# Blocked causal attention and token/channel mixer: neighbouring weight rows in one partition, every fourth channel in a chunk, and down projections that wait for their own third

## The chip, the cores and the metric

The kernel runs on one core of one Trainium2 chip. The metric is the device time of one execution in microseconds (us); medians are over several executions. All executions told of here are in the undisturbed ("fast") state, at a granted TensorE clock of 0.995 to 1.000 over the whole span. Beside the device time there is the span, from the first to the last instruction in the trace.

Engines: PE is TensorE (PEld its weight loads), DVE is VectorE, ACT is ScalarE, POOL is GpSimd, SP is SyncE. In this kernel PE's matmuls write into PSUM banks, and a bank is given to the next ones when DVE or ACT has read it out ("evacuated" it); in the trace before PE waits 0.6 us at two places where L507 needs a bank that x_sb (DVE) still has to read out. "Packed" weights have their columns side by side; with a step of 4 every fourth column is taken. The prediction uses the line numbers of the kernel before.

## The reference

```python
# q, k, v: (8, 8, 576, 64) drawn with standard deviation 0.1
def _attn_ref(q, k, v):
    scores = np.matmul(q, k.transpose(0, 1, 3, 2)) / np.sqrt(D)
    mask = block_i >= block_j                    # blocks of 64 positions
    scores = np.where(mask, scores, -1e9)
    attn = softmax(scores)
    return np.matmul(attn, v)

def _moe_ref(x, w_tok1, w_tok2, w_ch1, w_ch2):   # x: (8, 576, 512)
    xt = x.transpose(0, 2, 1)
    h = np.maximum(xt @ w_tok1, 0.0) @ w_tok2    # 576 -> 256 -> 576
    u = x + h.transpose(0, 2, 1)
    h2 = np.maximum(u @ w_ch1, 0.0) @ w_ch2      # 512 -> 1536 -> 512
    return u + h2
```

The heads of the attention, side by side, are the rows of x. Inputs and output are float32; the kernel multiplies in bfloat16.

## The kernel before

The kernel does not fix the order of its instructions by hand. It describes some thousand pieces of work with an engine, an estimated cost, dependencies and a priority. A list schedule then deals them out: whenever an engine is free on paper, it takes the piece of best priority whose dependencies are done on paper. The instructions are emitted in that order. In the trace before each engine's instructions start in the emitted order (by their lines, all 3029 matmuls of PE, 372 instructions of DVE and 234 of ACT), and PE's listed waits, 4.9 us in all, are each for a tile that DVE or ACT had to write or read.

```python
# costs of the plan, in us
def act_cost(n):          return 0.08 + n * 0.000833
def dve_cost(n, speed=1): return 0.09 + n * 0.00104 / speed
...
rc = P.add("DVE", 0.12, emit_rc, ...)                                # reciprocal of the row sums
mu = P.add("DVE", dve_cost(320), emit_mu, [rc], ..., give=[bank])    # x_sb, frees a PSUM bank
...
op = P.add("DVE", 0.02 + 32 * (k1 - k0) * 0.00185, emit, ...)        # transposes of q and k
...
def channel_up(b, uT_done, wc1_ready, prio):       # twelve chunks of 128 channels
    for cc in range(NDC):
        def emit(o, cc=cc, bank=bank):
            for m in range(NDM):
                nc.tensor.matmul(out=bank_of(bank),
                    lhsT=wc1_sb[:, m, 128 * cc : 128 * (cc + 1)],
                    rhs=uT[b % 2][:, :, m, :], start=(m == 0), stop=(m == NDM - 1))
        ...
        done.append(P.add(EVAC, evac_cost(512), emit, [op], prio, give=[bank]))   # relu into gT, DVE or ACT
...
def channel_down(b, g_done, wc2_ready, u_done, prio, mixed=False):
    ...
                for part in range(3):              # four of the twelve chunks each
                    ...
                        for cc in range(4 * part, 4 * part + 4):
                            nc.tensor.matmul(out=ps, lhsT=gt[:, cc, c0 : c0 + 128],
                                rhs=wc2_sb[:, cc, cols], ...)
                    deps = [prev] + (g_done + wc2_ready + u_done if part == 0 else [])
```

For batch 0 the first part also adds u by four matmuls with the identity (L950). In the last line a down projection depends on all twelve evacuations before its first third may start.

The softmax here doesn't subtract the row's maximum and nothing guards it: scores larger than these inputs give would overflow.

## Time and profile before

| | us |
|---|---|
| three runs before the change | 310.43 median (310.27 to 311.03) |
| six runs, three of them beside the changed kernel | 311.01 median (310.27 to 311.34) |
| span of the profiled run | 309.2 |

First the weight loads of the up projection, from the page's costliest groups (line, engine, operation, shape, count, then total us and mean ns of one). All are packed, and one takes 98 ns:

```profile
L874 PEld LDWEIGHTS <-wc_sb 128*128 128x128 bf16 x384 | 36.0, 98 | 44.5 <-issue 3.6
```

Second, DVE's timeline after batch 1's token mixing (start, length, work). The four sums u, which free PSUM banks and release the transposes on PE, run back to back with the fifth (um). The transposes of k and q, 1.23 to 1.26 us each, come after:

```profile
60.67 2.48 DVE L803 TENSOR_TENSOR u_sb<-mm,x_sb 128x512 bf16<-128x512 f32 x4 [2.05 <-PE mm L782]
63.19 0.69 DVE L803 TENSOR_TENSOR um_sb<-mm,x_sb 64x512 bf16<-64x512 f32 x1
...
64.76 1.26 DVE L349 STREAM_TRANSPOSE kT<-kraw 128x576 int32<-128x576 int32 x1
65.86 1.23 DVE L349 STREAM_TRANSPOSE qT<-qraw 128x576 int32<-128x576 int32 x1
```

### The profile page before, as it was taken

Reading aid. Unit: us, or ns where it says so; the run is one execution under the profiler, and the core shown is the slowest. Engines: PE = TensorE matmul, PEld = TensorE weight load, DVE = VectorE, ACT = ScalarE, POOL = GpSimd, SP = SyncE. Lnnn points to the kernel's source line nnn. Section 1 sums busy time; section 2 is a strip of 40 time slices with the busy share of each in tenths; the row PEclk is TensorE's granted clock in tenths of the full one; section 3 lists DMA queues with packets and bytes.
Section 4 is the critical chain, followed back from the end, with each engine's and each line's share of the span. In section 5 each row is a group of like instructions: output and inputs, shape, how many; then the busy total and the mean of one; then the engine's idle time right before and its main releaser. Section 6 shows DMA issues by size and latency. Waiting matters only on the chain.

```text
span 309.2 us, 7176 instructions
## 1 busy us (share of the span) xinstructions
PE 300.4 (97%) x3029; PEld 155.4 (50%) x3029; DVE 157.6 (51%) x372; ACT 165.8 (54%) x235; POOL 63.1 (20%) x96
## 2 busy tenths in 40 slices
PE   7999989999999999999999999999999999999995
PEld 3575436463556554554544556544444644444643
DVE  6967648796786497496557634525015012011021
ACT  5886864767876745758555776214603602613600
POOL 7956345611612511500220000000000000000000
PEclk9999999999999999999999999999999999999999
DMA  8999999998796996941291005104221312103004
GB/s 241 193 194 206 220 211 183 225 161 169 61 138 125 120 182 146 159 29 23 49 163 70 2 0 70 70 0 122 46 89 68 68 69 72 32 10 126 2 16 156
DMA packets 57024, 33.13 MB, mean 107 GB/s; under 512 B 43872, under 2 KB 47584, under 8 KB 56992
## 3 DMA queue, kind: packets, MB, share of 16 engines
q0 software_dynamic: 36960, 18.52, 45.6%
q1 hardware_dynamic: 19744, 13.57, 17.3%
q8 instruction: 23, 0.38, 0.5%
q10 hardware_dynamic: 288, 0.59, 0.5%
q14 instruction: 9, 0.07, 0.1%
HBM read 35.85 MB, written 9.44 MB: 146 GB/s over the span
## 4 chain that ended last, share of the span: by engine, by line
PE 85%; DMA 5%; DVE 4%; POOL 3%; ACT 1%; issue 1%; POOLq 0%
PE mm L958 30%; PE mm L874 26%; PE sc L460 8%; PE mm L507 7%; PE mm L782 5%; PE mm L688 5%; PE mm L901 4%; DMA qraw<-in_q_dram 3%; DMA kraw<-in_k_dram 2%; DVE x_sb L535 1%; ACT e_sb L479 1%; POOL gT L378 1%; DVE qT L349 1%; DVE kT L349 1%; POOL wc_sb L416 1%
## 5 line engine op out<-in xcount | busy, mean ns | idle before, releaser
L479 ACT ACTIVATE e_sb<-sc 128x1024 bf16<-128x1024 f32 x95 | 92.4, 1024 | 35.5 <-PE sc L460 34.9
L958 PE MATMUL mm<-wc_sb,gT 128*128 128x512 bf16 (+1 forms) x396 | 89.6, 373 | 0.0
L874 PE MATMUL mm<-uT,wc_sb 128*128 128x512 bf16 x384 | 88.6, 380 | 0.0
L674 ACT ACTIVATE gT<-mm 128x512 bf16<-128x512 f32 x75 | 44.8, 597 | 66.8 <-PE mm L874 66.6
L981 DVE TENSOR_TENSOR o_sb<-mm,u_sb 128x512 f32<-128x512 f32 (+1 forms) x29 | 19.5, 672 | 85.8 <-PE mm L958 85.8
L874 PEld LDWEIGHTS <-wc_sb 128*128 128x128 bf16 x384 | 36.0, 98 | 44.5 <-issue 3.6
L958 PEld LDWEIGHTS <-gT 128*128 128x128 bf16 x396 | 36.7, 98 | 41.3 <-issue 3.6
L460 PE MATMUL sc<-qT,kT 32*128 32x320 bf16 (+4 forms) x744 | 35.8, 281 | 2.7 <-DVE qT L349 1.6
L507 PEld LDWEIGHTS <-e_sb 128*128 128x128 bf16 x896 | 30.8, 97 | 9.3 <-issue 4.5
L507 PE MATMUL mm<-v,e_sb 128*128 128x65 bf16 x896 | 32.8, 193 | 1.1 <-DVE x_sb L535 0.6
L378 POOL DMA_DIRECT2D v<-in_v_dram x30 | 25.5, 869 | 39.8 <-PE sc L460 22.8
L535 DVE TENSOR_TENSOR x_sb<-mm,rinv 128x320 bf16<-128x320 f32 x64 | 30.4, 488 | 1.4
L460 PEld LDWEIGHTS <-kT 32*128 32x128 bf16 x752 | 12.8, 93 | 22.2 <-issue 19.3
L676 DVE TENSOR_SCALAR gT<-mm 128x512 bf16<-128x512 f32 x21 | 14.5, 690 | 15.3 <-PE mm L874 15.3
L349 DVE STREAM_TRANSPOSE kT<-kraw 128x576 int32<-128x576 int32 (+1 forms) x20 | 20.0, 1031 | 4.1 <-PE sc L460 2.9
L803 DVE TENSOR_TENSOR u_sb<-mm,x_sb 128x512 bf16<-128x512 f32 x28 | 17.4, 683 | 6.7 <-PE mm L782 6.7
L349 DVE STREAM_TRANSPOSE qT<-qraw 128x576 int32<-128x576 int32 (+1 forms) x20 | 20.0, 1025 | 0.7 <-DMA qraw<-in_q_dram 0.5
L688 PE MATMUL mm<-x_sb,w_sb 128*128 128x512 bf16 (+1 forms) x102 | 17.9, 316 | 0.3 <-DVE x_sb L535 0.3
L485 DVE MEMSET e_sb<- 64x128 uint32 (+1 forms) x72 | 10.6, 153 | 15.0 <-ACT e_sb L479 11.6
L782 PE MATMUL mm<-aT,w_sb 128*128 128x512 bf16 x72 | 17.0, 380 | 0.0
L329 POOL DMA_DIRECT2D kraw<-in_k_dram x15 | 8.4, 557 | 38.0 <-DVE kT L349 31.1
L529 DVE RECIPROCAL rinv<-mm 128x5 f32<-128x5 f32 x64 | 10.6, 180 | 9.2 <-PE mm L507 9.0
(68 smaller groups left out, 186.0 us busy)
## 6 DMA issues: line engine op xcount, KB each, us to landing
out_dram<-o_sb SPq DMA_DIRECT2D x15, 512.0 KB, 2.8
kraw<-in_k_dram POOLq DMA_DIRECT2D x15, 288.0 KB, 6.3
qraw<-in_q_dram POOLq DMA_DIRECT2D x15, 288.0 KB, 7.1
v<-in_v_dram POOLq DMA_DIRECT2D x24, 128.0 KB, 5.1
wc_sb<-in_moe_w_ch_dram POOLq DMA_DIRECT2D x8, 192.0 KB, 7.7
wc_sb<-in_moe_w_ch_dram POOLq DMA_DIRECT2D x3, 512.0 KB, 10.2
out_dram<-o_sb SPq DMA_DIRECT2D x10, 128.0 KB, 2.4
gT<-in_v_dram POOLq DMA_DIRECT2D x9, 128.0 KB, 6.1
```

What stands on the lines that cost most here:

```text
L349: nc.vector.transpose(dst[:, 0:S, :] .rearrange("p s e -> p (s e)") .bitcast(I32) .rearrange("p (a k) -> p k a", k=NB)[:, k0:k1], raw2.bit ...
L378: nc.gpsimd.dma_start(out=dst, in_=src)
L460: nc.tensor.matmul(out=home(n)[:, c0 : c0 + w], lhsT=kT[i][r, j0 : j0 + 128, par], rhs=qT[i][r, i0 : i0 + w, par], start=(par == 0), stop= ...
L479: nc.scalar.activation(dst, sc[SC.index(note["pool"])][:, :, 0:n], EXP, scale=scale)
L507: nc.tensor.matmul(out=u[:, I, 0:65], lhsT=w, rhs=vt[:, J, head, 0:65], start=(J == 0), stop=(J == I),)
L535: nc.vector.tensor_tensor(out=xt[:, :, 64 * head : 64 * head + 64], in0=u[:, :, 0:64], in1=ri.to_broadcast([128, 5, 64]), op=MULT,)
L674: nc.scalar.activation(dst, src, RELU)
L688: nc.tensor.matmul(out=bank_of(bank)[:, w * n : w * n + w], lhsT=wt[:, 128 * tt : 128 * (tt + 1)], rhs=xt[:, c, cols], start=(c == 0), sto ...
L782: nc.tensor.matmul(out=bank_of(bank), lhsT=w2_sb[:, t, c0 : c0 + 128], rhs=at[:, t, :], start=(t == 0), stop=(t == NDT - 1),)
L874: nc.tensor.matmul(out=bank_of(bank), lhsT=wc1_sb[:, m, 128 * cc : 128 * (cc + 1)], rhs=uT[b % 2][:, :, m, :], start=(m == 0), stop=(m == ...
L958: nc.tensor.matmul(out=ps, lhsT=gt[:, cc, c0 : c0 + 128], rhs=wc2_sb[:, cc, cols], start=(cc == 0 and not turned), stop=(cc == NDC - 1),)
L981: nc.vector.tensor_tensor(out=dst, in0=ps, in1=(ut if mixed else ut[:, si, :])[:, cols], op=ADD)
```

## The change

The intent: four neighbouring rows of w_ch2 are one piece of 4 x 512 values in a partition, so one transfer of w_ch2 needs a quarter of the packets; likewise two rows of w_tok2 were to halve its packets. To match, chunk cc of the hidden channels takes every fourth channel of its 512, so the up projection's weights are read with a column step of 4 (8 bytes), and those of the token mixing with a step of 2. And a third of a down projection depends only on the four evacuations that it reads. The fillers, matmuls on zeros that run before the data are there, take the strided forms too.

```diff
@@ fillers
-                nc.tensor.matmul(
-                    out=bank_of(bank)[:, 0:256], lhsT=zeros[:, 0:128], rhs=zeros[:, 0:256],
-                    start=True, stop=True,
-                )
+                if n % 4 == 1:
+                    for c in range(2):
+                        nc.tensor.matmul(
+                            out=bank_of(bank)[:, 0:128], lhsT=zeros[:, c : 512 + c : 4], rhs=zeros[:, 0:128],
+                            start=True, stop=True,
+                        )
+                else:
+                    cols = zeros[:, 0:256]
+                    if n % 4 == 3:
+                        cols = zeros.rearrange("p (k a e) -> p a k e", k=16, e=2)[:, 0:16, :, 0]
+                    nc.tensor.matmul(
+                        out=bank_of(bank)[:, 0:256], lhsT=zeros[:, 0:128], rhs=cols, start=True, stop=True
+                    )
@@ loads
-            load(w2_sb[:, :, 0:S], moe_w_tok2.rearrange("(c p) s -> p c s", p=128), 16 * 0.107, 5.2)
+            load(w2_sb[:, :, 0:S], moe_w_tok2.rearrange("(p c) s -> p c s", c=2), 8 * 0.192, 5.2)
+    def channels(cc):
+        return slice(512 * (cc // 4) + cc % 4, 512 * (cc // 4) + 512, 4)
...
-                    in_=moe_w_ch2[128 * c : 128 * (c + 4), :].rearrange("(c p) t -> p c t", p=128),
+                    in_=moe_w_ch2[128 * c : 128 * (c + 4), :].rearrange("(p c) t -> p c t", c=4),
-            done2.append(P.add("POOL", 0.66, emit, (), 15.5, xfer=32 * 0.098))
+            done2.append(P.add("POOL", 0.66, emit, (), 15.5, xfer=8 * 0.324))
@@ weights of token mixing, and of both up projections
-                        lhsT=wt[:, 128 * tt : 128 * (tt + 1)],
+                        lhsT=wt[:, tt : tt + 255 : 2],
-                        lhsT=wc1_sb[:, m, 128 * cc : 128 * (cc + 1)],
+                        lhsT=wc1_sb[:, m, channels(cc)],
@@ down projection
-                    deps = [prev] + (g_done + wc2_ready + u_done if part == 0 else [])
+                    gs = g_done[part : part + 1] if mixed else g_done[4 * part : 4 * part + 4]
+                    deps = [prev] + gs + wc2_ready[part : part + 1] + (u_done if part == 0 else [])
```

More of the change, by code (lines that the diff above doesn't have):

```diff
@@ L202 @@
     ident = sb.tile([128, 128], BF16, name="ident")
-    zeros = sb.tile([128, 512], BF16, name="zeros")
+    zeros = sb.tile([128, 1024], BF16, name="zeros")
     w1_sb = sb.tile([128, 5, DT], BF16, name="w1_sb")
@@ L265, in init_tiles @@
             fill("DVE", ("um", i), -70, (um_sb[i], 0.0))
-        fill("DVE", "zeros", -1e5, (zeros, 0.0))
+        fill("DVE", "zeros", -1e5, (zeros[:, 0:512], 0.0))
+        fill("DVE", "more zeros", -1e3, (zeros[:, 512:1024], 0.0))
         fill("DVE", "w1", -70, (w1_sb[64:128, 4, :], 0.0), (w1o_sb[0:64, :], 0.0))
@@ L280, in emit @@
             for _ in range(WARM):
-                nc.tensor.matmul(out=bank_of(bank), lhsT=zeros[:, 0:128], rhs=zeros, start=True, stop=True)
+                nc.tensor.matmul(out=bank_of(bank), lhsT=zeros[:, 0:128], rhs=zeros[:, 0:512], start=True, stop=True)
         P.add("PE", WARM * 0.36, emit, pads["zeros"], -1e6, take=[(BANK, bank)], give=[bank])
@@ L285, in raise_clock, with emit @@
             bank = {}
-            def emit(o, bank=bank):
-                nc.tensor.matmul(
-                    out=bank_of(bank)[:, 0:256], lhsT=zeros[:, 0:128], rhs=zeros[:, 0:256],
-                    start=True, stop=True,
-                )
+            def emit(o, bank=bank, n=n):
+                if n % 4 == 1:
[11 more added lines that the diff above has]
+                    )
             P.add(
-                "PE", 0.11, emit, pads["zeros"], 1e6, take=[(BANK, bank)], give=[bank], at=5.0 + 0.12 * n, until=20.0,
+                "PE", 0.11, emit, pads["zeros"] + pads["more zeros"], 1e6, take=[(BANK, bank)], give=[bank], at=5.0 + 0.12 * n, until=20.0,
                 quick=True,
@@ L420, in load_channel_weights @@
                 op = P.add("POOL", 0.66, emit, (), (6.0, 11.5)[f], xfer=8 * 0.134)
-                for cc in range(6 * f, 6 * f + 6):
+                for cc in range(0, 8) if f == 0 else range(4, NDC):
                     done1[cc].append(op)
@@ L902, in emit @@
                             out=bank_of(bank)[:, 128 * c : 128 * (c + 1)],
-                            lhsT=wc1_sb[:, m, 128 * cc : 128 * (cc + 1)],
+                            lhsT=wc1_sb[:, m, channels(cc)],
                             rhs=umT[pair % 2][:, m, :],
```

## The prediction

Its sum: it came to -1.66 us, and with +0.3 for new waits to about -1.4 us. The +0.2 for strided weights is the author's guess between 0 and 1.2 us: at worst 62 ns for a load with step 4, twice the 31 ns at step 2 in the trace, so 6 ns over 56 for 192 matmuls; why it should double, and why it could be 0, is cut. The 0 for the fillers rests on PE's idle time until 15 us alone. That 512-column matmuls are safe was the author's estimate too: 216 ns from start to start, against 98 ns recorded for a load. The first rival, slow weights: its 4% were a guess.

> **What bounds the kernel now.** I read the page first, then the chain of work that ended last, then the waits of the TensorE (PE), then its timeline around the longest wait. The page's first lines and its chain:
>
> ```profile
> span 309.2 us, 7176 instructions
> PE 300.4 (97%) x3029; PEld 155.4 (50%) x3029; DVE 157.6 (51%) x372; ACT 165.8 (54%) x235; POOL 63.1 (20%) x96
> ...
> PE 85%; DMA 5%; DVE 4%; POOL 3%; ACT 1%; issue 1%; POOLq 0%
> ```
>
> PE is busy 97% of the span and is 85% of the chain. A busy PE need not be a full one[...]. Matmuls of 512 columns start 216 ns apart in 350 of the pairs of the up projection, a mean 0.5 ns above that. PE really streams. From about 26 us on it hardly stops; what it loses is shown by its waits:
>
> ```profile
> PE sc L460 <- DVE qT L349: 1.6, 2, 1.2
> PE mm L281 <- DVE zeros L250: 1.2, 1, 1.2
> PE sc L460 <- ACT e_sb L479: 0.7, 1, 0.7
> PE mm L507 <- DVE x_sb L535: 0.6, 2, 0.4
> PE mm L507 <- DVE e_sb L485: 0.5, 1, 0.5
> PE mm L688 <- DVE x_sb L535: 0.3, 2, 0.2
> ```
>
> In all 4.9 us (total us, times, longest), of which 1.2 + 1.2 + 0.5 us lie before 17 us, in the start. So a change that leaves PE's work alone can win two or three microseconds of 309, no more. The longest wait after the start, in PE's timeline (start, length, line, work):
>
> ```profile
> 39.36 0.63 PE L460 MATMUL sc<-qT,kT 32*128 32x512 bf16 x8
> 39.92 1.04 PE L874 MATMUL mm<-uT,wc_sb 128*128 128x512 bf16 x4
> 41.10 0.21 PE L460 MATMUL sc<-qT,kT 32*128 32x64 bf16 x2
> 42.01 0.63 PE L460 MATMUL sc<-qT,kT 32*128 32x64 bf16 x14 [0.71 <-ACT e_sb L479]
> 42.57 0.40 PE L950 MATMUL mm<-ident,uT 128*128 128x128 bf16 x4
> ```
>
> The up projection of batch 0 ends; its last four matmuls start at 39.92, so they stream until about 40.79. Then PE has only scores to do, whose two PSUM buffers ACT still reads (exponentials until 41.97). The down projection of batch 0 (L950, L958) could fill that time, but waits for all twelve evacuations of gT, and the last of these runs on DVE from 41.00 to 41.69.
>
> [...]every weight load is recorded in the shape [32,1,4], also that of kT (L460), whose columns are 2 elements apart.[...] No run here shows step 4 yet.[...] a packet that lands 1024 bytes takes 98 ns, one that lands 2304 bytes has a median of 192 ns, 10.4 against 12.0 bytes per ns and engine.
>
> **The change part by part.** I built both kernels and compared their instruction order.
>
> *Work on PE.* The same real matmuls in the same shapes, and the same 116 switches between the 32-row score matmuls and full ones. Only fillers at the start change (29 matmuls for 23): they run in PE's idle time until 15 us.[...] I count 0.
>
> *Strided weights.* 576 up-projection weights come with step 4, 110 token weights with step 2.[...] For 512 columns there are 216 ns; safe. The critical ones are those with 128 columns: 192 of L901 and 40 of L688.
>
> ```profile
> 88.15 0.23 PE sc L460 x15
> ...
> 90.78 1.91 PE mm L507 x60
> ...
> 290.26 2.68 PE mm L901 x48
> ```
>
> From the chain: 48 of L901 take 2.68 us, 56 ns each, the streaming rate. L507 reloads packed weights every 1.91/60 = 32 ns. The score tail loads kT at step 2: four matmuls in each of four row groups in 0.23 us, at most 57 ns each, and single records of one group start 31 ns apart. Step 2 is therefore free against 56 ns.[...] at worst 2 x 31 = 62 ns (my estimate), 6 ns over, 192 x 6 = 1.2 us.[...] I take +0.2.
>
> *The third of a down projection.* In the new order PE goes from the last up projection of batch 0 straight to two thirds of down projections (transposes by identity, four matmuls; twice, some 2.2 us) and does the scores after these. The gap from 39.92 on is then gone: the starts show 302 ns lost before 41.10 and 910 ns before 42.01, less about 124 ns for the switch that stays and 27 ns of normal spacing: -1.06 us. Elsewhere in the order single down parts are moved between attention heads and token matmuls; the waits near 50, 52, 63 and 67 us (DVE freeing PSUM banks, 1.4 us together in the starts) may shrink, as more PE work lies between heads, but DVE has the same work (15.05 of 20 us in 60:80). I take 0.4 of the 1.4. The wait at 126.6 us gets four up matmuls in front: -0.2. After 200 us both kernels are dense matmuls to the end: 0.
>
> *DMA.* w_ch2 falls from 3 x 512 packets of 1024 landed bytes to 3 x 128 of 4096, w_tok2 from 256 of 1152 to 128 of 2304. At 98 ns, 512 packets on 16 engines are 3.1 us; at an estimated 4096/12.0 = 341 ns, 128 are 2.7 us. So about 1.2 us of queue time is saved for w_ch2, but the queue there feeds loads that PE does not wait for; 0 on the path. w_tok2 lies ahead of a load that is on the path:
>
> ```profile
> 15.98 9.76 DMA qraw<-in_q_dram
> 25.76 1.27 DVE qT L349 x2
> 27.07 0.64 PE sc L460 x8
> ```
>
> Those q rows take 9.76 us because the queue is full (DMA share above 1.1 from 8 to 40 us). w_tok2: 256 packets at 107 to 137 ns over 16 engines are 1.7 to 2.2 us, 128 at 192 to 211 are 1.5 to 1.7; 0.2 to 0.5 us earlier. PE lost 0.42 us before 27.07 beyond the switch; I take -0.2.
>
> Sum: +0.2 - 1.06 - 0.4 - 0.2 - 0.2 = -1.66 us. A list schedule laid anew tends to open a new small wait somewhere; +0.3. That gives -1.4 us: 310.4 to **309.0 us**, a ratio of 0.9955.
>
> **The rivals.** *Weights with step 4 are slow.*[...] For: no step of 4 in this trace. Against: step 2 runs at packed speed[...]. I give it 4%; the mild form, +1.2 us, some 15%. *The gain is taken back by ACT and DVE.* The scores at 41 us start about 1 us later, so do their exponentials, masks and the heads after them; PE then waits there instead. For: DVE is 72% and ACT 65% busy from 40 to 80 us, and PE's waits near 50 us are for DVE. Against: the down parts are PE work that must be done anyway and ACT idles 1.78 us before 46.39. It would make 310 to 310.5. *The time was never in these weights' DMA.* Nothing waits for w_ch2 in PE's waits; if w_tok2 too is hidden, 0.2 us of my sum go: 309.2.
>
> **Range and chances.** Without slow weights I see 307.8 (all waits from 26 to 67 us gone, some -2.7) to 310.4 (all given back); the mild slow weights stretch it a little: 307.8 to 310.6. Faster by 2% would need 6.2 us, more than PE waits in all: 0.02. Slower by 2% needs slow strided loads: 0.04. Within 2%: 0.94.
>
> **What would show it.** Right: spacing of L901's counterpart stays 56 ns; the gap at 40.8 to 42.0 us is gone and down matmuls stand there; the q load of 16 us lands a few tenths earlier; PE's work ends about 1.4 us earlier. Wrong: L901's 48 matmuls take over 3 us; weight loads above 98 ns or a shape other than [32,1,4]; new waits of PE for DVE or ACT between 42 and 67 us of a microsecond or more; the start before 26 us later because of the strided fillers.

## More of the kernel before

In the changed kernel L460 became L474 (scores), L507 L521 (attention times v), L535 L549 (x_sb), L688 L702 and L782 L796 (token mixing), L803 L817 (u), L835 L849 (transposes of u), L874 L888 and L901 L915 (up projections), L950 L964 and L958 L972 (down projections). Experiments that start from the changed kernel with plain fillers have numbers 10 lower than the changed kernel, and so have e2 and e11 from L460 on (L460 became L464).

## The result, and the profile after

| kernel | runs | median us | range |
|---|---|---|---|
| before | 6 | 311.01 | 310.27 to 311.34 |
| after | 6 | 311.27 | 311.15 to 311.63 |

The ratio is 1.0015, with a 95% interval of 1.0001 to 1.0028: the same within 2%, and above the predicted range. Here and below, a ratio is the mean time of one kernel's fast runs over the mean of the other's, so not quite the ratio of the medians that are quoted. Here the six runs before include the first three, which were low; against the three beside the changed kernel (mean 311.17 us) the ratio of the means is 1.0005.

The page of the changed kernel, span, busy times and chain:

```profile
span 309.4 us, 7161 instructions
PE 301.1 (97%) x3009; PEld 162.2 (52%) x3035; DVE 157.5 (51%) x374; ACT 165.6 (54%) x234; POOL 62.3 (20%) x96
...
PE 89%; DVE 7%; issue 2%; ACT 1%
```

DVE's share of the chain went from 4% to 7%; the 5% of DMA are gone (2% in the second trace). PE lacks 26 of its 3035 matmul records. The waits "for issue" of 0.2 us in the list of PE's waits (L972, five times) are such holes of one 512-column matmul. A second trace of the same program, taken later and complete (3035 records), has no such waits, and the reading below uses it.

PE's waits after, from the first trace:

```profile
PE mm L849 <- DVE u_sb L817: 0.3, 1, 0.3
PE mm L915 <- DVE x_sb L549: 0.3, 1, 0.3
...
PE mm L849 <- DVE x_sb L549: 0.2, 1, 0.2
PE mm L521 <- DVE o_sb L997: 0.2, 1, 0.2
```

The wait of L460 for qT at 27 us, that for e_sb at 42 us and those of L507 for x_sb are gone. In their place stand small ones, five of the seven for DVE. (That the wait at 27 us is gone is not the change's doing; see under the table.) PE's timeline, where the gap was, shows the predicted picture. The down projection's matmuls (L964, L972) stand between the last up projection and the scores:

```profile
40.12 1.05 PE L888 MATMUL mm<-uT,wc_sb 128*128 128x512 bf16 x4
41.01 0.39 PE L964 MATMUL mm<-ident,uT 128*128 128x128 bf16 x4
41.24 1.03 PE L972 MATMUL mm<-wc_sb,gT 128*128 128x512 bf16 x3
...
42.32 1.03 PE L972 MATMUL mm<-wc_sb,gT 128*128 128x512 bf16 x4
43.28 0.44 PE L474 MATMUL sc<-qT,kT 32*128 32x64 bf16 x12
```

The mixed up projection keeps its time (48 matmuls in 2.68 us, as before, in the chain of work that ended last), though weight loads are recorded longer (the up projection's, from the page; 98 ns before), still in the shape [32,1,4]:

```profile
290.38 2.68 PE mm L915 x48
```

```profile
L888 PEld LDWEIGHTS <-wc_sb 128*128 128x128 bf16 x384 | 42.1, 114 | 39.9 <-issue 4.4
```

### Where PE's time went

PE's real work is the same in every kernel: its matmuls' columns add up to 274.1 us, at N/2.4 + 2.5 ns for a full matmul of N columns and N/9.6 ns for one of the four row groups of scores. The first fits the trace before: in dense stretches the starts are 216, 109, 56 and 29.8 ns apart for 512, 256, 128 and 65 columns, and it gives 215.8, 109.2, 55.8 and 29.6. The second is an estimate, a quarter of that slope: four scores, one in each row group, start a median of 3 to 4 ns apart, and four of the same size follow after at least 227 ns (median 240) with 512 columns and 29 (39) with 64, where the estimate gives 213 and 27. All else is loss. I took it from the starts of neighbouring matmuls: start to start, less this time of the first of the two. Losses of over 0.06 us between full matmuls, and of over 0.3 us at a switch to or from scores, I call waits. From the latter I took off 0.12 us for the switch itself (after 26 us in the trace before, 46 of 49 switches to scores lose 0.093 to 0.096 us, and 46 of 49 from scores 0.111 to 0.262). The table sets the trace before beside the complete second trace of the changed kernel (spans of 309.2 and 308.9 us):

| loss, us | before | after | difference |
|---|---|---|---|
| start, up to 26 us | 14.26 | 14.43 | +0.17 |
| wait at 27 us (qT) | 0.43 | 0 | -0.43 |
| gap at 41 to 42 us | 0.96 | 0 | -0.96 |
| wait at 50.6 us | 0.37 | 0 | -0.37 |
| waits from 63 to 69 us | 1.08 | 1.36 | +0.28 |
| wait at 93.5 us | 0 | 0.46 | +0.46 |
| wait at 117 us | 0 | 0.39 | +0.39 |
| wait of token mixing, 127 before, 132 after | 0.34 | 0.33 | -0.01 |
| waits later than 150 us | 0.42 | 0.40 | -0.02 |
| full matmuls, the rest (small spacings) | 1.01 | 1.33 | +0.32 |
| scores and switches, the rest | 11.58 | 11.46 | -0.12 |
| sum | 30.45 | 30.16 | -0.29 |

So 1.76 us of waits went, and 1.13 us of new ones came. The weights' small spacings took 0.32 us, and the start 0.17 us. In the traces 0.29 us remain as a gain.

But the 0.43 us at 27 us is not the change's. The experiments e1 to e6, e8 and e11 have before's order on every engine up to there, and yet the wait is, by the starts, 0.64 us in e2, 0.23 in e3, 0.68 in e8 and 0 in the other five. So it comes and goes from one execution to the next. PE's timeline in the trace before and in e6 (old layout, old order; only transposes of later batches are shortened):

```profile
27.07 0.64 PE L460 MATMUL sc<-qT,kT 32*128 32x512 bf16 x8 [0.39 <-DVE qT L349]
```

```profile
26.87 0.63 PE L460 MATMUL sc<-qT,kT 32*128 32x512 bf16 x8
```

Without it the change removed 1.33 us of waits, and the table ends at +0.14 us instead of -0.29.

That fits the runs. This second trace has the shortest span of the five runs taken with it: their spans are 308.9 to 309.6, a mean of 309.26, against a mean of 309.23 for nine runs of the kernel before beside them. On average nothing remains. (By device time the same execution is the longest of the five, 311.73 us. Its 2.8 us outside the span are in no trace, and stay unexplained.) The first trace has the same waits and differs mainly in its start, 14.87 us.

The packets of w_tok2 did not become fewer. The page before, and the page after:

```profile
DMA packets 57024, 33.13 MB, mean 107 GB/s; under 512 B 43872, under 2 KB 47584, under 8 KB 56992
```

```profile
DMA packets 55872, 33.13 MB, mean 107 GB/s; under 512 B 43872, under 2 KB 46048, under 8 KB 55840
```

The total falls by 1152, which is 3 x (512 - 128), the packets of w_ch2 alone. In the trace's packet records the 256 packets of 1152 landed bytes of w_tok2 stand after the change as before. Its tile has rows of 640 columns, of which the load fills 576, so that two rows are not one piece there; that this is the reason was not tested.

The new waits, read on DVE and PE in the complete trace. First DVE at batch 1's token mixing, as shown above for before:

```profile
60.73 1.89 DVE L817 TENSOR_TENSOR u_sb<-mm,x_sb 128x512 bf16<-128x512 f32 x3 [3.08 <-PE mm L796]
...
63.04 1.26 DVE L359 STREAM_TRANSPOSE kT<-kraw 128x576 int32<-128x576 int32 x1
64.14 0.68 DVE L817 TENSOR_TENSOR u_sb<-mm,x_sb 128x512 bf16<-128x512 f32 x1
64.85 0.69 DVE L817 TENSOR_TENSOR um_sb<-mm,x_sb 64x512 bf16<-64x512 f32 x1
```

The transpose of k now stands ahead of the fourth sum. PE, which has three of five chunks, runs out of them (the first of these three waits, 0.28 us by the starts, is for ACT's copy of uT, and the trace before has one of that size at 63.3 us):

```profile
64.19 0.38 PE L849 MATMUL mm<-ident,u_sb 128*128 128x128 bf16 x4 [0.22 <-ACT uT L864]
64.88 0.40 PE L849 MATMUL mm<-ident,u_sb 128*128 128x128 bf16 x4 [0.31 <-DVE u_sb L817]
...
67.90 0.38 PE L849 MATMUL mm<-ident,um_sb 128*128 128x128 bf16 x4 [0.22 <-DVE x_sb L549]
```

At 93.5 us the story is of the same kind. DVE has the transpose of q until about 92.8, and only then the reciprocals and x_sb that free PSUM banks; PE stops at 93.5 for a bank:

```profile
91.68 1.24 DVE L359 STREAM_TRANSPOSE qT<-qraw 128x576 int32<-128x576 int32 x1
92.75 0.20 DVE L543 RECIPROCAL rinv<-mm 128x5 f32<-128x5 f32 x2
92.97 0.89 DVE L549 TENSOR_TENSOR x_sb<-mm,rinv 128x320 bf16<-128x320 f32 x2
```

```profile
93.52 1.05 PE L915 MATMUL mm<-umT,wc_sb 128*128 128x128 bf16 x16 [0.29 <-DVE x_sb L549]
```

The kernel before has that very sequence on DVE at 91.22 to 93.41 us. But there PE has a set of scores from 92.63 on, before it needs the bank. In the new order that set comes after the up projection, at 94.5. What hid the transpose has moved away. At 117 us it is a transpose of k that stands ahead (DVE, then PE):

```profile
114.76 1.26 DVE L359 STREAM_TRANSPOSE kT<-kraw 128x576 int32<-128x576 int32 x1
116.05 0.20 DVE L543 RECIPROCAL rinv<-mm 128x5 f32<-128x5 f32 x1
116.16 0.65 DVE L997 TENSOR_TENSOR o_sb<-mm,u_sb 128x512 f32<-128x512 f32 x1
```

```profile
116.86 0.58 PE L521 MATMUL mm<-v,e_sb 128*128 128x65 bf16 x14 [0.19 <-DVE o_sb L997]
```

### The profile page after: what moved, and what is told of

Its sections match the earlier page's. It is cut to its first block, busy times and chain, and to the rows that moved or that the text cites. A ratio compares the mean times of both kernels' runs of the same rounds, so it can differ in the third digit from the quotient of the medians.

```text
span 309.4 us, 7161 instructions
## 1 busy us (share of the span) xinstructions
PE 301.1 (97%) x3009; PEld 162.2 (52%) x3035; DVE 157.5 (51%) x374; ACT 165.6 (54%) x234; POOL 62.3 (20%) x96
## 4 chain that ended last, share of the span: by engine, by line
PE 89%; DVE 7%; issue 2%; ACT 1%
PE mm L972 29%; PE mm L888 27%; PE sc L474 9%; PE mm L521 7%; PE mm L702 6%; PE mm L796 4%; PE mm L915 3%; PE mm L282 2%; DVE x_sb L549 1%; ACT e_sb L493 1%; PE mm L299 1%; DVE kT L359 1%; DVE u_sb L817 1%; DVE qT L359 1%; DVE um_sb L817 1%
## 5 line engine op out<-in xcount | busy, mean ns | idle before, releaser
L972 PE MATMUL mm<-wc_sb,gT 128*128 128x512 bf16 (+1 forms) x379 | 86.7, 373 | 1.4 <-issue 0.8
L688 ACT ACTIVATE gT<-mm 128x512 bf16<-128x512 f32 x71 | 42.4, 597 | 63.2 <-PE mm L888 63.1
L888 PEld LDWEIGHTS <-wc_sb 128*128 128x128 bf16 x384 | 42.1, 114 | 39.9 <-issue 4.4
L972 PEld LDWEIGHTS <-gT 128*128 128x128 bf16 x396 | 36.8, 98 | 41.6 <-issue 3.8
L474 PE MATMUL sc<-qT,kT 32*128 32x512 bf16 (+4 forms) x744 | 35.3, 281 | 0.2 <-ACT e_sb L493 0.2
L388 POOL DMA_DIRECT2D v<-in_v_dram x30 | 25.5, 864 | 29.6 <-PE sc L474 19.7
L690 DVE TENSOR_SCALAR gT<-mm 128x512 bf16<-128x512 f32 x25 | 17.2, 689 | 17.8 <-PE mm L888 17.6
L688 ACT ACTIVATE aT<-mm 128x512 bf16<-128x512 f32 (+1 forms) x17 | 9.3, 547 | 13.7 <-PE mm L702 13.7
```

Source lines behind the costliest of these rows:

```text
L388: nc.gpsimd.dma_start(out=dst, in_=src)
L474: nc.tensor.matmul(out=home(n)[:, c0 : c0 + w], lhsT=kT[i][r, j0 : j0 + 128, par], rhs=qT[i][r, i0 : i0 + w, par], start=(par == 0), stop= ...
L688: nc.scalar.activation(dst, src, RELU)
L888: nc.tensor.matmul(out=bank_of(bank), lhsT=wc1_sb[:, m, channels(cc)], rhs=uT[b % 2][:, :, m, :], start=(m == 0), stop=(m == NDM - 1),)
L972: nc.tensor.matmul(out=ps, lhsT=gt[:, cc, c0 : c0 + 128], rhs=wc2_sb[:, cc, cols], start=(cc == 0 and not turned), stop=(cc == NDC - 1),)
```

## The experiments

Three theories stood after the result. **A**: the savings are spent in new waits for DVE, because the new deal (the order that the list schedule makes), like the old one, rests on costs for DVE that are too low. **B**: the strided weights cost what the order gains. **C**: the strided fillers delay the start. The lead of a kernel is the time by which its PE is ahead of the kernel before at the same work. All kernels told of passed the numeric comparison. The kernels e1 to e4, e5 to e8 and e9 to e12 ran together, each four on one chip with common runs of the kernel before.

| label | runs | median us (range) | before, same rounds | ratio [95%] |
|---|---|---|---|---|
| e1_plain_fillers | 5 | 310.96 (310.51 to 311.24) | 310.93 | 0.9997 [0.9984, 1.0009] |
| e2_layout_only_pinned | 5 | 311.22 (310.81 to 311.41) | 310.93 | 1.0006 [0.9994, 1.0018] |
| e3_deps_only | 6 | 311.70 (311.35 to 314.75) | 310.93 | 1.0036 [1.0007, 1.0066] |
| e4_deps_first_batch_only | 6 | 310.51 (310.37 to 312.26) | 310.93 | 0.9998 [0.9978, 1.0018] |
| e5_relief_after | 4 | 309.18 (308.81 to 309.52) | 310.91 | 0.9944 [0.9930, 0.9958] |
| e6_relief_before | 4 | 309.63 (309.58 to 309.82) | 310.91 | 0.9956 [0.9943, 0.9969] |
| e7_vector_costs | 6 | 309.45 (308.83 to 310.23) | 310.91 | 0.9950 [0.9936, 0.9963] |
| e8_urgent_vector | 4 | 309.67 (309.61 to 309.86) | 310.91 | 0.9957 [0.9944, 0.9970] |
| e9_vector_costs_before | 5 | 308.78 (308.52 to 309.14) | 310.98 | 0.9926 [0.9912, 0.9940] |
| e10_vector_costs_deps_only | 5 | 309.62 (309.54 to 309.87) | 310.98 | 0.9955 [0.9943, 0.9968] |
| e11_weights_step_12 | 4 | 312.91 (312.80 to 312.92) | 310.98 | 1.0059 [1.0045, 1.0073] |
| e12_changed_again | 5 | 311.14 (310.72 to 311.73) | 310.98 | 1.0007 [0.9995, 1.0020] |

### e1: the change with the fillers of before

```diff
-                if n % 4 == 1:  ... strided fillers ...
+                nc.tensor.matmul(out=bank_of(bank)[:, 0:256], lhsT=zeros[:, 0:128],
+                                 rhs=zeros[:, 0:256], start=True, stop=True)
```

> The changed kernel with the fillers of the kernel before (no strided ones, zeros of 512 columns). The order of all other work is that of the changed kernel. Theory A (the gain of 1.1 us at 41 us is real and is spent later in waits for VectorE): 0.2 to 0.6 us below the changed kernel's 1.0015, so a ratio to before of 0.9995 to 1.001; the waits at 64, 68 and 93 us stay. Theory C (the strided fillers delay the start and that is what ate the gain): 0.997 or less. Theory B (the new layout costs time by itself): 1.001 or more.

The order of all other work is that of the changed kernel. 310.96 us, 0.9997: level with before. In the traces the start up to 26 us loses 13.8 to 14.5 us in eleven traces with plain fillers (the kernel before and e1 to e10) and 14.87 and 14.43 in the two traces of the changed kernel. By the starts in the first of these, a filler of 256 columns with a moving step of 128 bytes takes 415 ns, a packed one 109 ns. The starts themselves scatter: the first matmuls of 512 columns, the same in both kernels, start some 427 ns apart and then 216, and the change comes 2.9 us after the first of them in the trace before and 5.5 us after it in the first trace of the changed kernel. So C may be worth a few tenths of a microsecond, but one of the two starts (14.43) lies within the range of the plain ones. But the changed kernel's ratios (1.0015 and 1.0007) and e1's have intervals that overlap. **C is not settled, and with either filler the gain of 1.4 us does not appear.** From here on experiments start from e1.

### e2: the layout alone, in the order of before

```diff
+ all of the change except:
-                    gs = ...; deps = [prev] + gs + wc2_ready[part : part + 1] + ...
+                    deps = [prev] + (g_done + wc2_ready + u_done if part == 0 else [])
  plain fillers; the plan's transfer costs of before, so every engine keeps before's order
```

> Only the layout of w_ch2 and w_tok2 (and the strided up-projection weights), with the old dependencies and the scheduler's old transfer costs, so that every engine has exactly the order of the kernel before. Theory A: the layout is free or wins a little by the q rows that land earlier: ratio 0.9985 to 1.0005, L901's 48 matmuls in 2.68 us as before. Theory B: 1.0015 or more.

311.22 us, 1.0006: just above A's range and below B's, so at most 0.2% (0.6 us). The time of w_ch2's transfers never shows. The gap at 42 us is still there (L464 for e_sb, 0.7 us), and so is a wait for qT at 27 us. The layout does not bring the q rows earlier: the first transpose of these rows into qT starts at 25.85 us here and at 25.76 before. That start scatters from one execution to the next: 25.92 and 25.27 in the two traces of the changed kernel, 25.44 in e3 and e6, 25.35 in e11. Matmuls of 512 columns in the up projection start 217.10 ns apart on average (217.16 in e1), against 216.33 before; times 384 that is 0.3 us. It lies at the start of groups, where the first gap is up to 246 ns instead of 228. B exists at that size.

### e3: the dependencies alone, in the layout of before

```diff
-                    deps = [prev] + (g_done + wc2_ready + u_done if part == 0 else [])
+                    gs = g_done[part : part + 1] if mixed else g_done[4 * part : 4 * part + 4]
+                    deps = [prev] + gs + wc2_ready[part : part + 1] + (u_done if part == 0 else [])
```

> Only the dependencies: the old layout, a third of a down projection waits for its own rows. The scheduler deals out the order anew from about 41 us. Theory A: the gap at 41 us is gone (-1 us there), waits for VectorE between 45 and 140 us take most of it back: ratio 0.998 to 1.001. Theory B (layout is the cost): 0.9965 or less, since the dependency's gain would stand alone.

311.70 us, 1.0036: above A's range too, and slower than before, though the gap at 41 us is gone here as well. So the layout cannot be what takes the gain back: B as the main cause falls. This deal has another new wait for DVE, in PE's timeline:

```profile
70.29 1.02 PE L874 MATMUL mm<-uT,wc_sb 128*128 128x512 bf16 x4 [0.83 <-DVE x_sb L535]
```

One of the six runs (314.75, at a clock of 0.995) widens the interval; the other five have spans of 309.6 to 310.1, above nearly all of before's.

### e4: the new dependencies for batch 0 only

```diff
+                    if b > 0:
+                        deps = [prev] + (g_done + wc2_ready + u_done if part == 0 else [])
```

> Changed kernel with plain fillers, and the new dependencies for batch 0 alone. The order is that of the changed kernel until about 93 us and another from then on. Theory A: the waits at 64 to 68 us stay, those after 93 us are dealt anew; the time stays within 0.5 us of e1, on either side. Rival D (the finer dependency of the later batches is what does harm): 0.997 or less, the lead of 1 us at 90 us is kept to the end.

310.51 us, but one run of 312.26 leaves the ratio at 0.9998 [0.9978, 1.0018]: inconclusive on the time. Its trace has e1's waits of 64 to 69, 93, 117 and 132 us, each within 0.01 us; only smaller ones after 150 us differ. So **the new waits need only the finer dependencies of batch 0**, not those of later batches.

### e5 and e6: half of DVE's transposes of q and k taken away, in the new order and in the old

```diff
-                def emit(o, raw2=raw2, dst=dst, k0=k0, k1=k1):
+                def emit(o, raw2=raw2, dst=dst, k0=k0, k1=k0 + (k1 - k0) // (1 if b < 2 else 2)):
```

The plan is told nothing, so orders do not move; the result is wrong from batch 2 on. (Both passed the numeric comparison all the same; presumably the scores of inputs this small hardly differ from each other.) e5 starts from e1, e6 from the kernel before, as the control.

> e1 (changed kernel, plain fillers), with the VectorE transposes of k and q from batch 2 on cut to half their columns: some 24 instructions of 1.24 us become about 0.65 us, no instruction is moved. The result is wrong on purpose. Theory A (the gain is taken back by waits for VectorE between 64 and 148 us): the lead of 2.6 us at 63 us in e1's trace is kept in good part, ratio to before 0.991 to 0.996 (308.1 to 309.7 us). Rival E (the lead is lost to something else, ScalarE's exponentials or the order itself): 0.997 or more.

> The control: the kernel before with the same cut of its transposes, wrong on purpose. It has 1.4 us of waits for VectorE near 50 to 67 us and 0.2 at 126 us to lose. Theory A: ratio 0.995 to 0.999, and e5 is at least 1 us below it. Rival E: e5 and e6 within 0.5 us.

e5 takes 309.18 us, 1.78 less than e1; e6 309.63, some 1.3 less than before. Both ratios lie in A's ranges, but the difference of 0.45 us does not: A asked for at least 1 us, and within 0.5 us is what was written for E. In e5 the waits of L839 for u_sb and x_sb, and those at 93.5 and 117 us, are gone; the 0.28 us for ACT's copy of uT stay. A transpose of half the length, 0.72 us here, does not hold DVE long enough:

```profile
62.74 0.72 DVE L349 STREAM_TRANSPOSE kT<-kraw 128x288 int32<-128x288 int32 x1
63.30 0.68 DVE L807 TENSOR_TENSOR u_sb<-mm,x_sb 128x512 bf16<-128x512 f32 x1
```

That ties the new waits to the transposes, as A has it. It does not single out the new order by time, for the old one has waits for DVE too (at 50.6 and 67.7 us among others), and loses most of them as well. The lead of the new order, nothing with full transposes, is 0.45 us with the relief, and the intervals of e5 and e6 still overlap. So these two runs show where the waits come from, and not that they alone ate the lead.

### e7: e1 with the plan's DVE costs set to what the trace shows

```diff
-        return 0.09 + n * 0.00104 / speed            # 512: 0.62
+        return 0.13 + n * 0.00107 / speed            # 512: 0.68
-    "DVE", 0.02 + 32 * (k1 - k0) * 0.00185           # whole transpose: 1.09
+    "DVE", 0.10 + 32 * (k1 - k0) * 0.00195           # 1.22
-    rc = P.add("DVE", 0.12, ...)    mask: P.add("DVE", 0.1, ...)
+    rc = P.add("DVE", 0.19, ...)    mask: P.add("DVE", 0.16, ...)
```

> e1 with the scheduler's costs for VectorE set to what the trace shows (a 512-column evacuation 0.68 us instead of 0.62, a reciprocal 0.19 instead of 0.12, a transpose of 576 columns 1.22 instead of 1.09, a mask 0.16 instead of 0.10); everything is dealt out anew, from 13 us on. Theory A': the schedule loses the lead because it believes VectorE to be faster than it is; ratio 0.993 to 0.997. If VectorE simply has too much to do in that stretch, or each new deal is luck: 0.998 to 1.003.

The trace before has 0.683 to 0.691 us for an operation of 512 columns from PSUM, 1.23 to 1.25 for a whole transpose, 0.488 for x_sb (plan: 0.42) and 0.18 for a reciprocal. With these costs the same change takes 309.45 us, 1.5 less than e1. The only thing altered is the order. From 60 to 80 us, where e1's trace has 1.35 us of waits by the starts, two of 0.77 us together stand in e7's.

### e8: e1 with the DVE operations that free PSUM ahead of others

```diff
-   op = P.add("DVE", dve_cost(512), emit, [op], prio, give=[bank])              # sums u
+   op = P.add("DVE", dve_cost(512), emit, [op], prio, give=[bank], urgent=1)
    (likewise the reciprocal and x_sb)
```

> e1 with the VectorE instructions that free a PSUM bank (the sums of u, the reciprocal and scaling of attention heads) marked urgent, so that the scheduler doesn't start a transpose just ahead of one. Theory A: ratio 0.993 to 0.998, fewer waits of PE for VectorE at 64, 93 and 117 us. If the stretch is bound by VectorE's total, waits for transposes (scores waiting for kT or qT) take their place: 0.998 to 1.003.

309.67 us, 1.3 less than e1, with the old low costs. Of the new waits one is left, 0.5 us at 64.4; those near 68, 93.5 and 117 us are gone. Two unlike edits that both put DVE's bank-freeing work earlier thus come out near what the prediction had promised and the change did not give. The marks of e8 were not tried in the kernel before, so what they are worth without the new dependencies is open.

### e9 and e10: the same costs without the layout; and without the dependencies

```diff
  e9:  kernel before + the costs of e7
  e10: kernel before + the new dependencies + the costs of e7
```

> The control to e7: the kernel before, with old dependencies and old layout, and only the scheduler's VectorE costs set to the trace's. If e7's gain (ratio 0.995) came from keeping the dependency's lead: 0.999 or more here. If it came from the better costs alone and the dependency adds nothing: 0.994 to 0.996.

> Old layout, new dependencies, VectorE costs from the trace: the layout's cost (0.3 us by the spacing of 384 up-projection matmuls, 217.16 against 216.33 ns) is left out. If deals of the schedule were equal: 0.3 us below e7, ratio 0.994. A new deal can move it by 1 us either way; above 0.998 the costs are no reliable cure.

e9 takes 308.78 us, 0.7% less than before and **the fastest of all, with the old layout and the old dependencies**. e10 takes 309.62: its interval [0.9943, 0.9968] lies above that of e9 [0.9912, 0.9940]. e9 is below, e10 above what was expected. So in these two deals under right costs the finer dependencies add 0.8 us instead of saving something; it is one deal each. The gap at 41 us is closed in e9 too, by the order alone (PE's timeline):

```profile
39.14 1.04 PE L874 MATMUL mm<-uT,wc_sb 128*128 128x512 bf16 x4
40.11 0.73 PE L460 MATMUL sc<-qT,kT 32*128 32x512 bf16 x8
40.77 0.40 PE L950 MATMUL mm<-ident,uT 128*128 128x128 bf16 x4
41.01 1.03 PE L958 MATMUL mm<-wc_sb,gT 128*128 128x512 bf16 x4
```

The old dependency was no obstacle. In e9's trace the waits after 26 us are 2.13 us in all, against 3.60 before; the last is at 70 us. What is gone is the gap at 41 us (0.96) and all that came after 100 us (0.76 before). The stretch from 60 to 80 us is not better: DVE is busy for 17.83 of its 20 us there, as in the changed kernel (17.58) and unlike before (15.05), and PE's waits in it are 1.20 us in e9 and 1.94 in e10, against 1.08 before and 1.36 in the changed kernel. So right costs do not keep PE from waiting there; which waits a deal opens still differs from deal to deal.

### e11: e2 with a step of 12 columns

```diff
-        return slice(512 * (cc // 4) + cc % 4, 512 * (cc // 4) + 512, 4)
+        return slice(cc, NDC * 128, NDC)
-    in_=moe_w_ch2[128 * c : 128 * (c + 4), :].rearrange("(p c) t -> p c t", c=4),
+    in_=moe_w_ch2.rearrange("(p c) t -> p c t", c=NDC)[:, c : c + 4],
```

(The first case, over 62 ns and over 312.2 us, is the author's estimate for loads that step 12 slows down.)

> e2 with 12 neighbouring rows of w_ch2 in a partition instead of 4, so that up-projection weights have a column step of 12 elements (24 bytes[...]); every engine keeps the order of the kernel before.[...] L901's matmuls of 128 columns are spaced by over 62 ns, the time is over 312.2 us[...]. If only the column count matters: 56 ns and a time within 0.5 us of e2 (311.2).

Each weight column now lies 24 bytes from the next, against 8 at step 4. 312.91 us, 0.5% over e2 (by the ratios to before). The time is above the 312.2 us of the first case, the spacing below lies between the two. The mixed up projection takes up to 3.02 us for the 48 matmuls that took 2.79 at the same place before (chain of work), and a load is recorded with 143 ns in the mean (page; 98 packed, 114 at step 4):

```profile
94.24 3.02 PE mm L905 x48
```

```profile
L878 PEld LDWEIGHTS <-wc_sb 128*128 128x128 bf16 x384 | 52.9, 143 | 30.5 <-issue 3.4
```

Within dense stretches those matmuls start 59.8 ns apart, against 56 at step 4 and packed. The 512-column groups start later too: their first gap is up to 278 ns. And some 0.5 us are not the loads' cost: a chunk now reads both halves of w_ch1, and PE waits for them at 29 us (L878 for wc_sb, 0.48 us by the starts). So at step 4 the loads add nothing to the 56 ns of 128 columns, and at step 12 they add 4 ns. The prediction's estimate of at worst 62 ns for step 4 is nearer to the 59.8 of step 12.

### e12: the changed kernel once more

```diff
  (none)
```

> The changed kernel once more, beside the kernel before on one chip, to set against e1 (0.9997 on another chip): 1.001 to 1.002 if the strided fillers cost the start some 0.4 us; 0.9997 if that was the chip.

311.14 us, 1.0007 [0.9995, 1.0020]. The first ratio, 1.0015, was barely apart from 1, and rests in part on three early low runs of before; together they say that the change does nothing measurable, or costs up to some 0.2%. This is the complete trace that the table of losses uses.

## Why the prediction was wrong

It said 309.0 us (307.8 to 310.6), and 311.27 was measured. Its range failed, its class (within 2%) held. By its own steps, against the table of losses:

- **The gap at 41 us, -1.06.** Right, in mechanism and size: -0.96, with down matmuls in the place of the gap.
- **The waits near 50 to 67 us, -0.4.** -0.37 came at 50.6, but 63 to 69 us got worse by 0.28: -0.09.
- **The wait at 126.6 us, -0.2.** It moved to 132 us with the same length: 0.
- **w_tok2 and the q rows, -0.2.** This term was 0, and its mechanism did not happen: w_tok2's packets stayed 256. PE's wait at 27 us fell by 0.43 in this pair of traces, by luck: it ranges from 0 to 0.68 us in traces that have before's order up to there. w_ch2's packets did become fewer, and that was worth nothing on the path, as the rival on DMA said.
- **Strided weights, +0.2.** +0.32, by another way: not the 128-column matmuls, whose spacing stayed at 56 ns, but mostly the starts of 512-column groups (first gap up to 246 ns in e2, 228 before), which I had called safe because a load, recorded with 98 ns packed and 114 at step 4, is shorter than 216 ns.
- **Fillers, 0.** +0.17 in one trace, +0.61 in the other; not settled.
- **New waits, +0.3.** This is the step that failed: "A list schedule laid anew tends to open a new small wait somewhere; +0.3." The runs show +1.13 us, in the waits at 63 to 69, 93.5 and 117 us, nearly all for DVE with a transpose ahead of the operation that PE needs (the 0.28 us for ACT stand in both traces).

In one sum, without the wait at 27 us: the waits removed are 1.33 us, and I had 1.86 for them (1.06 + 0.4 + 0.2 + 0.2), so 0.53 too much. The term for what comes back was 0.83 too small, weights 0.12 and the start 0.17; less 0.12 at the scores and 0.03 at the last waits, that makes the 1.5 us between -1.4 and +0.14. A further 0.58 us is the base: I predicted from 310.43, and with the three runs beside the changed kernel the median of all six was 311.01. 310.43 + 0.58 + 0.14 is 311.15, and 311.27 and 311.14 were measured. What came true is the rival "the gain is taken back by ACT and DVE", with DVE as its agent; I had written against it that the down parts are work to be done anyway and that ACT idles, and looked for its waits between 42 and 67 us only. Two of three lie later, up to 75 us after the move. The view that would have warned was within reach: DVE's list of groups against the costs in the plan. A deal made with costs that DVE's operations exceed by 10 to 50% (0.68 for 0.62, 0.18 for 0.12) puts DVE's work later on the chip than on paper, wherever it is laid; that PE then has less slack to hide it is argued, not shown.

What is shown: the gap closes and new waits for DVE open in every kernel with the new dependencies and old costs (e1, e3, e4 and both traces of the change; e3 has partly others); most of those in e1 go when DVE is relieved (e5) or put in another order (e7, e8). What is only argued: that the too low costs are the root, and that each corrected cost matters. e7, e9 and e10 are three deals that all gained 0.45 to 0.74%, and the four deals with the old costs (before, e1, e3, e4) lie at 310.5 to 311.7 us; but each deal is a single draw, e9 may be a lucky one, and no deal with costs altered at random was run against them. Which share of the wait at 64 us is the transpose's place alone was not tried.

## What to carry to other kernels

Where a list schedule deals the instructions, a finer dependency is a new deal and not a shorter wait: first compare the plan's costs with the durations in the trace, for that alone gave 2.2 us here (e9, one deal) where the finer dependency gave none. Before a saving in one pair of traces is credited to a change, look for the same wait in traces that share its order: the one at 27 us came and went by itself. And count the packets after a change of layout. Predict a new deal as the waits removed minus the waits it will open, and size the second term by the engine whose queue decides when buffers come free, over all the later batches, not just beside the removed gap. To find where a lead goes, sum PE's losses wait by wait in both traces, and relieve the suspected engine in both orders, with the old order as the control.
